# Attention of a batch in three visits of both head halves by a third of the tokens, in place of four of one half by one half; the last numerators left to the next tile

## Chip, cores, metric

One core of one Trainium2 chip. The metric is the device time of one execution in microseconds (us); lower is better.

## The reference

Attention over keys and values pooled in eights, followed by a gated feed-forward block over all tokens. Tokens 4608, model width 512, hidden width 2048.

```python
# shortened
k_p = k.reshape(8, 8, 72, 8, 64).mean(axis=3)       # batch, head, pooled row, 8, 64
v_p = v.reshape(8, 8, 72, 8, 64).mean(axis=3)
scores = scale * np.matmul(q, k_p.transpose(0, 1, 3, 2))   # 576 x 72 per head
attn = np.exp(scores - max)
attn = attn / (np.sum(attn, axis=-1, keepdims=True) + 1e-09)
x = (attn @ v_p) -> tokens x 512
h = x @ w_in;  g = h * sigmoid(h);  out = g @ w_out
```

## The kernel before

The tokens pass in nine tiles of 512. Each tile has a first half ("up": x @ w_in, SiLU) and a second half ("down": the product with w_out). From tile 1 on, both halves use a seven-product scheme in place of eight; that is where the sums on DVE come from. Attention of batch t+1 is put into the second half of tile t: a list of pieces, each with a position, and between large product number i-1 and i of that half the pieces with position up to i are emitted. Every engine works its own list in the order of emission.

A piece of attention is one of three groups of small matmuls. Four of them sit side by side in the array, as each uses 32 rows or 32 columns.

```python
def scores(b, g, f):            # g: half of the heads, f: half of the tokens
    sc = [ps_tile([128, 512], FP32, "at", "sc_ps")[:SP, :HS] for s in range(4)]
    for c in range(2):
        for s in range(4):
            rows = slice(32 * s, 32 * (s + 1))
            nc.tensor.matmul(sc[s], lhsT=kz[b % 2][rows, g, c, :],
                rhs=st["qT"][rows, g, f * QF : (f + 1) * QF, c, :], ...)
    es = mid.tile([SP, 4, HS], BF16, tag="es", bufs=4, name="es")
    for s in range(4):
        nc.scalar.activation(es[:, s, :], sc[s], func=AF.Exp, scale=score_scale)
# denominators(b, g, f): 4 matmuls of 288 columns with ones, then 1/x as exp(-ln x) on ACT
# numerators(b, g, f):   8 matmuls of 288 columns, then 2 multiplications by 1/x on DVE into xT
...
q_at = [15, 16, 17, 49] if t > 1 else [24, 25, 26, 49] if t else [82, 84, 86, 88]
# the first three q transposes stand in "up", the fourth (position 49) in "down"
f_down.append((10, lambda: pool_v(a)))                       # tiles 2 on: additions for v
...
for stage in range(2):
    f_down.append((100, lambda stage=stage: pool_k(a + 1, stage)))   # additions for k
f_up.append((0, lambda: load_q(a + 1)))
f_up.append((1, lambda: load_one(a + 1, "k")))     # first half of the rows, from SyncE
f_up.append((2, lambda: load_rest(a + 1, "k")))    # second half added by the DMA, from GpSimd
f_down.append((11, lambda: load_one(a + 1, "v")))
f_down.append((12, lambda: load_rest(a + 1, "v")))
...
visits = [(f, g) for f in range(2) for g in range(2)]
sc_at, den_at, nu_at = (1, 28, 56, 77), (28, 46, 69, 89), (46, 69, 89, 93)   # tiles 1 to 6
sc_at, den_at, nu_at = (1, 14, 22, 30), (14, 22, 30, 38), (42, 47, 52, 57)   # tile 0
```

k and v are summed in eights: the first half of the rows is loaded by SyncE's queue, the second is added to it by an accumulating DMA from GpSimd (which waits for the first), and three additions on DVE do the rest.

The softmax here doesn't subtract the row's maximum and nothing guards it: scores larger than these inputs give would overflow.

## Time and profile before

| | before |
|---|---|
| time, median | 290.5 us (290.41 to 291.13) |
| PE busy | 281.2 of 288.6 us |
| matmuls recorded | 2578 |
| DVE busy | 226.8 us |

How to read it: PE is the bound, so a change helps if it takes time from PE or fills a stop of PE. DVE, busy four fifths of the time, is the engine whose order can stop PE. The lines are in the prediction. A **visit** is one run of small matmuls between large ones. A **lap** is the time from the first large product of one tile's second half to that of the next tile's; laps leave out the start, whose length differs by about 1 us between runs of any kernel (see the last section).

### The profile page before, as it was taken

To read this page: it belongs to the slowest core of one execution; us is meant where nothing else is said; L and a number is where in the kernel's file an instruction comes from. 1 tells how busy PE (TensorE), PEld (TensorE's weight loads), DVE (VectorE), ACT (ScalarE), POOL (GpSimd) and SP (SyncE) were. 2 spreads that over 40 slices of the span, in tenths; PEclk is the share of its full clock that TensorE was granted. 3 is DMA by queue.
4 is the path that set the end of the run, shared out by engine and by line. 5 is a ranking of instruction groups with operands and counts; after the bars stand their busy time and mean duration, and the time that the engine had idled before them with its cause. 6 is when DMAs were issued, how large, how long until landed. Compare 5 with 4: busy or idle time off the path is not lost.

```text
span 288.6 us, 6600 instructions
## 1 busy us (share of the span) xinstructions
PE 281.2 (97%) x2578; PEld 189.9 (66%) x2597; DVE 226.8 (79%) x417; ACT 187.9 (65%) x401; POOL 52.2 (18%) x68
## 2 busy tenths in 40 slices
PE   7989999999999999999999999999999999999995
PEld 2448434465667676657788767676777667786684
DVE  4986844989789796979698879887988876746783
ACT  1768675568656877578767866786679657425700
POOL 8744316501020011101200106203000000000000
PEclk9999999999999999999999999999999999999999
DMA  7999999893758565875995495979830023005004
GB/s 214 276 278 215 232 301 151 221 206 55 145 82 187 127 91 76 133 179 123 137 182 166 61 138 81 164 156 163 149 82 2 2 65 83 1 2 140 6 2 145
DMA packets 35295, 37.67 MB, mean 131 GB/s; under 512 B 9952, under 2 KB 27616, under 8 KB 35264
## 3 DMA queue, kind: packets, MB, share of 16 engines
q0 software_dynamic: 21760, 20.86, 43.3%
q1 hardware_dynamic: 12928, 15.48, 22.0%
q10 hardware_dynamic: 576, 0.92, 0.9%
q8 instruction: 20, 0.33, 0.5%
q14 instruction: 11, 0.09, 0.1%
HBM read 36.70 MB, written 9.44 MB: 160 GB/s over the span
## 4 chain that ended last, share of the span: by engine, by line
PE 91%; DVE 2%; ACT 2%; DMA 2%; issue 1%; DVEq 0%
PE hp_ps L518 24%; PE o_psP L623 15%; PE o_psQ L623 15%; PE u_psQ L460 6%; PE u_psP L460 6%; PE o_psR L623 5%; PE o_ps L550 4%; PE sc_ps L330 4%; PE nu_ps L370 3%; PE den_ps L347 3%; PE u_psR L460 2%; DMA raw<-in_k_dram 2%; PE warm_ps L672 1%; ACT es L338 1%; PE kz_ps L295 1%
## 5 line engine op out<-in xcount | busy, mean ns | idle before, releaser
L518 PE MATMUL hp_ps<-xT,w_in_sb 128*128 128x512 bf16 (+3 forms) x398 | 80.5, 338 | 1.2 <-ACT h_T L524 0.4
L524 ACT ACTIVATE h_T<-hp_ps 128x512 bf16<-128x512 f32 (+2 forms) x95 | 51.4, 545 | 33.1 <-PE hp_ps L518 31.9
L623 PEld LDWEIGHTS <-h_sum 128*128 128x128 bf16 x640 | 60.4, 98 | 15.2 <-issue 6.1
L583 DVE TENSOR_TENSOR h_sum<-h_T 128x1024 bf16<-128x1024 bf16 (+1 forms) x72 | 50.9, 743 | 7.0 <-ACT h_T L524 7.0
L518 PEld LDWEIGHTS <-w_in_sb 128*128 128x128 bf16 x412 | 39.3, 98 | 24.9 <-issue 1.5
L338 ACT ACTIVATE es<-sc_ps 72x288 bf16<-72x288 f32 x128 | 41.4, 402 | 12.6 <-PE sc_ps L330 12.5
L378 DVE TENSOR_TENSOR xT<-nu_ps,rec 128x288 bf16<-128x288 f32 x64 | 25.8, 450 | 13.2 <-PE nu_ps L370 13.0
L460 PEld LDWEIGHTS <-w_sum 128*128 128x128 bf16 x300 | 29.3, 98 | 7.7
L623 PEld LDWEIGHTS <-h_T 128*128 128x128 bf16 x256 | 23.5, 98 | 6.7 <-issue 4.3
L468 ACT ACTIVATE h_T<-c_sb 128x512 bf16<-128x512 f32 x30 | 18.8, 628 | 10.8 <-DVE c_sb L492 10.8
L152 DVE STREAM_TRANSPOSE qT<-q_bf 128x576 bf16<-128x576 bf16 x32 | 22.9, 753 | 0.0
L181 POOL DMA_DIRECT2D raw<-in_k_dram x5 | 7.0, 1405 | 75.1 <-DVE h_sum L583 37.7
L356 ACT ACTIVATE lnd<-den_ps 128x288 f32<-128x288 f32 x30 | 12.3, 411 | 10.8 <-PE nu_ps L370 5.8
L273 DVE TENSOR_TENSOR raw<-raw 128x384 f32<-128x384 f32 (+3 forms) x20 | 12.4, 619 | 8.0 <-DMA raw<-in_v_dram 4.4
L623 PE MATMUL o_psP<-w_out_sb,h_sum 128*128 128x256 bf16 x128 | 17.6, 273 | 0.0
L623 PE MATMUL o_psQ<-w_out_sb,h_sum 128*128 128x256 bf16 x128 | 17.6, 273 | 0.0
L623 PE MATMUL o_psQ<-w_sum,h_T 128*128 128x256 bf16 x128 | 17.5, 274 | 0.0
L623 PE MATMUL o_psP<-w_sum,h_sum 128*128 128x256 bf16 x128 | 17.0, 273 | 0.0
L623 PE MATMUL o_psR<-w_sum,h_sum 128*128 128x256 bf16 x128 | 16.7, 273 | 0.0
L623 PE MATMUL o_psP<-w_sum,h_T 128*128 128x256 bf16 x128 | 16.7, 273 | 0.0
L530 POOL DMA_DIRECT2D out_dram<-o_sb x1 | 0.6, 628 | 82.3 <-issue 82.3
L623 PE MATMUL o_psQ<-w_sum,h_sum 128*128 128x256 bf16 x128 | 15.4, 273 | 0.0
(77 smaller groups left out, 426.8 us busy)
## 6 DMA issues: line engine op xcount, KB each, us to landing
out_dram<-o_sb SPq DMA_DIRECT2D x128, 64.0 KB, 2.5
q_bf<-in_q_dram POOLq DMA_DIRECT2D x6, 576.0 KB, 11.4
raw<-in_k_dram SPq DMA_DIRECT2D x6, 512.0 KB, 5.5
raw<-in_k_dram POOLq DMA_DIRECT2D x5, 576.0 KB, 8.8
raw<-in_v_dram POOLq DMA_DIRECT2D x5, 576.0 KB, 8.7
raw<-in_v_dram SPq DMA_DIRECT2D x5, 512.0 KB, 6.4
w_in_sb<-in_moe_w_in_dram POOLq DMA_DIRECT2D x8, 256.0 KB, 8.7
w_out_sb<-in_moe_w_out_dram POOLq DMA_DIRECT2D x4, 512.0 KB, 13.5
```

The costliest lines, as they stand in the source:

```text
L152: nc.vector.transpose(out=st["qT"][:, a, f * QF : (f + 1) * QF].rearrange("r i c p -> r (i c p)"), in_=st["q_bf"][:, a, f * n : (f + 1) * n],)
L273: nc.vector.tensor_add(out=raw[..., :w], in0=raw[..., :w], in1=raw[..., w : 2 * w])
L330: nc.tensor.matmul(sc[s], lhsT=kz[b % 2][rows, g, c, :], rhs=st["qT"][rows, g, f * QF : (f + 1) * QF, c, :], start=(c == 0), stop=(c == 1),)
L338: nc.scalar.activation(es[:, s, :], sc[s], func=AF.Exp, scale=score_scale)
L356: nc.scalar.activation(lnd, den_ps[:, :HS], func=AF.Ln)
L378: nc.vector.tensor_mul(out=xT[:, 2 * g + c, cols], in0=nu[c][:, :HS], in1=rec)
L460: nc.tensor.matmul(ps[bank][:, u, :], lhsT=w[:, kk, 128 * u : 128 * (u + 1)], rhs=x[:, kk, :], start=first and u == 0 and kk == 0, stop=kk ...
L468: nc.scalar.activation(h_T[:, g : g + 2, j * NQ : (j + 1) * NQ], src, func=AF.Silu)
L518: nc.tensor.matmul(hp_ps[:, r0:r1], lhsT=w_in_sb[:, kk, g * 128 : (g + 1) * 128], rhs=xT[:, kk, x0 : x0 + r1 - r0], start=(kk == 0), stop= ...
L524: nc.scalar.activation(h_T[:, g, n0 : n0 + n], hp_ps[:, :n], func=AF.Silu)
L583: nc.vector.tensor_tensor(out=h_sum[n][:, ks, :], in0=quarter(*a, ks), in1=quarter(*b, ks), op=op)
L623: nc.tensor.matmul(ps[b][:, c, :], lhsT=left(n, kt, c), rhs=W_OUT[n][:, kt, :], start=b not in begun, stop=kt == k1 - 1, skip_group_check= ...
```

## The change

Intent: each batch needs three scores, three denominators and three numerators in place of four of each. A visit handles both head halves of a third of the tokens: scores 16 matmuls of 192 columns, denominators 4 of 384, numerators 16 of 192. Where two groups meet at one position they share a visit, and the numerators of the last third are put behind the first numerators of the next tile. The middle third needs the last quarter of q, so that transpose moves up from 49 to 8.

```diff
+    QV = QI // 3
+    def third(n):
+        return tuple((g, n * QV, (n + 1) * QV) for g in range(2))
-    def scores(b, g, f):
+    def scores(b, segs):
...
-    visits = [(f, g) for f in range(2) for g in range(2)]
+    visits = [third(n) for n in range(3)]
...
-            q_at = [15, 16, 17, 49] if t > 1 else [24, 25, 26, 49] if t else [82, 84, 86, 88]
+            q_at = [15, 16, 17, 8] if t > 1 else [24, 25, 26, 8] if t else [82, 84, 86, 88]
...
-                f_to.append((q_at[n], lambda n=n: q_transpose(a, n // 2, n % 2)))
+                f_to.append((q_at[n], lambda n=n: q_transpose(a, n % 2, n // 2)))
...
-                sc_at, den_at, nu_at = (1, 28, 56, 77), (28, 46, 69, 89), (46, 69, 89, 93)
+                sc_at, den_at, nu_at = (1, 31, 75), (31, 56, 97), (56, 97, 101)
             else:
-                sc_at, den_at, nu_at = (1, 14, 22, 30), (14, 22, 30, 38), (42, 47, 52, 57)
+                sc_at, den_at, nu_at = (1, 16, 30), (16, 30, 44), (44, 55, 56)
...
-                if n < 3 or not 3 <= t < B - 2:
+                if n < 2 or not 0 < t < B - 2:
...
-                if n == 0 and 3 < t < B - 1:
-                    f_down.append((nu_at[n], lambda: numerators(a - 1, 1, 1)))
+                if n == 0 and 1 < t < B - 1:
+                    f_down.append((nu_at[n], lambda: numerators(a - 1, visits[2])))
```

More of the change, by code (lines that the diff above doesn't have):

```diff
@@ L69 @@
     DH = D // 2
+    VW = max(HS, 2 * S // 3)
     score_scale = float(1.0 / (D ** 0.5) / POOL)
@@ L320, in copy_v, with part, width, seg_cols @@
         copy(out=batches[b]["vp"][:, hs, :], in_=batches[b]["v_ps"][:SP, hs, :])
-    def scores(b, g, f):
-        st = batches[b]
-        sc = [ps_tile([128, 512], FP32, "at", "sc_ps")[:SP, :HS] for s in range(4)]
-        for c in range(2):
-            for s in range(4):
-                rows = slice(32 * s, 32 * (s + 1))
-                nc.tensor.matmul(
-                    sc[s],
-                    lhsT=kz[b % 2][rows, g, c, :],
-                    rhs=st["qT"][rows, g, f * QF : (f + 1) * QF, c, :],
-                    start=(c == 0), stop=(c == 1),
-                )
-        es = mid.tile([SP, 4, HS], BF16, tag="es", bufs=4, name="es")
+    def part(g, f):
+        return ((g, f * QF, (f + 1) * QF),)
+    QV = QI // 3
+    def third(n):
+        return tuple((g, n * QV, (n + 1) * QV) for g in range(2))
+    def width(segs):
+        return QP * sum(i1 - i0 for _, i0, i1 in segs)
+    def seg_cols(segs):
+        o = 0
+        for g, i0, i1 in segs:
+            n = QP * (i1 - i0)
+            yield g, i0, i1, slice(o, o + n)
+            o += n
+    def scores(b, segs):
+        st = batches[b]
+        w = width(segs)
+        sc = [ps_tile([128, 512], FP32, "at", "sc_ps")[:SP, :w] for s in range(4)]
+        for g, i0, i1, cs in seg_cols(segs):
+            for c in range(2):
+                for s in range(4):
+                    rows = slice(32 * s, 32 * (s + 1))
+                    nc.tensor.matmul(
+                        sc[s][:, cs],
+                        lhsT=kz[b % 2][rows, g, c, :],
+                        rhs=st["qT"][rows, g, i0:i1, c, :],
+                        start=(c == 0), stop=(c == 1),
+                    )
+        es = mid.tile([SP, 4, VW], BF16, tag="es", bufs=4, name="es")[:, :, :w]
         for s in range(4):
             nc.scalar.activation(es[:, s, :], sc[s], func=AF.Exp, scale=score_scale)
-        st[f"es{g}{f}"] = es
-    def denominators(b, g, f, on_dve=False):
+        st["es", segs] = es
+    def denominators(b, segs, on_dve=False):
         st = batches[b]
-        es = st[f"es{g}{f}"]
+        w = width(segs)
+        es = st["es", segs]
         den_ps = ps_tile([128, 512], FP32, "at", "den_ps")
@@ L347, in denominators, with numerators @@
             nc.tensor.matmul(
-                den_ps[32 * s : 32 * (s + 1), :HS],
+                den_ps[32 * s : 32 * (s + 1), :w],
                 lhsT=ones, rhs=es[:, s, :], start=True, stop=True,
             )
-        rec = mid.tile([128, HS], FP32, tag="rec", bufs=4, name="rec")
+        rec = mid.tile([128, VW], FP32, tag="rec", bufs=4, name="rec")[:, :w]
         if on_dve:
-            nc.vector.reciprocal(rec, den_ps[:, :HS])
+            nc.vector.reciprocal(rec, den_ps[:, :w])
         else:
-            lnd = mid.tile([128, HS], FP32, tag="lnd", name="lnd")
-            nc.scalar.activation(lnd, den_ps[:, :HS], func=AF.Ln)
+            lnd = mid.tile([128, VW], FP32, tag="lnd", name="lnd")[:, :w]
+            nc.scalar.activation(lnd, den_ps[:, :w], func=AF.Ln)
             nc.scalar.activation(rec, lnd, func=AF.Exp, scale=-1.0)
-        st[f"rec{g}{f}"] = rec
-    def numerators(b, g, f, tags=("at", "at")):
+        st["rec", segs] = rec
+    def numerators(b, segs, tags=("at", "at")):
         st = batches[b]
-        c0 = b * S % NX + f * HS
-        cols = slice(c0, c0 + HS)
-        es = st.pop(f"es{g}{f}")
-        rec = st.pop(f"rec{g}{f}")
+        w = width(segs)
+        g0, i0, i1 = segs[0]
+        c0 = b * S % NX + i0 * QP
+        cols = slice(c0, c0 + (i1 - i0) * QP)
+        es = st.pop(("es", segs))
+        rec = st.pop(("rec", segs))
         nu = []
@@ L368, in numerators @@
             nu_ps = ps_tile([128, 512], FP32, tags[c], "nu_ps")
-            for s in range(4):
-                nc.tensor.matmul(
-                    nu_ps[32 * s : 32 * (s + 1), :HS],
-                    lhsT=st["vp"][:, 4 * g + s, c::2],
-                    rhs=es[:, s, :],
-                    start=True, stop=True,
-                )
+            for g, _, _, cs in seg_cols(segs):
+                for s in range(4):
+                    nc.tensor.matmul(
+                        nu_ps[32 * s : 32 * (s + 1), cs],
+                        lhsT=st["vp"][:, 4 * g + s, c::2],
+                        rhs=es[:, s, cs],
+                        start=True, stop=True,
+                    )
             nu.append(nu_ps)
+        ng = len(segs)
         for c in range(2):
             nc.vector.tensor_mul(
-                out=xT[:, 2 * g + c, cols], in0=nu[c][:, :HS], in1=rec
+                out=xT[:, 2 * g0 + c : 2 * (g0 + ng - 1) + c + 1 : 2, cols],
+                in0=nu[c][:, :w].rearrange("r (g n) -> r g n", g=ng),
+                in1=rec.rearrange("r (g n) -> r g n", g=ng),
             )
@@ L712 @@
     q_transpose(0, 0, 0)
-    scores(0, 0, 0)
+    scores(0, part(0, 0))
     slot_sums("k", 1)
@@ L719 @@
     warm_up(2)
-    scores(0, 1, 0)
-    denominators(0, 0, 0)
+    scores(0, part(1, 0))
+    denominators(0, part(0, 0))
     slot_sums("v", 0)
@@ L725 @@
     copy_v(0, 0, act_copy)
-    denominators(0, 1, 0)
+    denominators(0, part(1, 0))
     q_transpose(0, 0, 1)
-    scores(0, 0, 1)
+    scores(0, part(0, 1))
     slot_sums("v", 1)
     warm_up(1)
-    numerators(0, 0, 0, ("mm", "at"))
+    numerators(0, part(0, 0), ("mm", "at"))
     warm_up(2)
@@ L736 @@
     warm_up(2)
-    numerators(0, 1, 0, ("mm", "at"))
-    scores(0, 1, 1)
+    numerators(0, part(1, 0), ("mm", "at"))
+    scores(0, part(1, 1))
     warm_up(2)
@@ L764 @@
             items += [(g, 0, NTT) for g in range(GA, KG)]
-            f_up += [(1, lambda: denominators(0, 0, 1, on_dve=True))]
-            f_up += [(5, lambda: denominators(0, 1, 1, on_dve=True))]
-            f_up += [(13, lambda: numerators(0, 0, 1))]
-            f_up += [(17, lambda: numerators(0, 1, 1))]
+            f_up += [(1, lambda: denominators(0, part(0, 1), on_dve=True))]
+            f_up += [(5, lambda: denominators(0, part(1, 1), on_dve=True))]
+            f_up += [(13, lambda: numerators(0, part(0, 1)))]
+            f_up += [(17, lambda: numerators(0, part(1, 1)))]
         else:
@@ L843 @@
             if t:
-                sc_at, den_at, nu_at = (1, 28, 56, 77), (28, 46, 69, 89), (46, 69, 89, 93)
+                sc_at, den_at, nu_at = (1, 31, 75), (31, 56, 97), (56, 97, 101)
             else:
-                sc_at, den_at, nu_at = (1, 14, 22, 30), (14, 22, 30, 38), (42, 47, 52, 57)
-            for n, (f, g) in enumerate(visits):
-                f_down.append((den_at[n], lambda f=f, g=g: denominators(a, g, f)))
-                f_down.append((sc_at[n], lambda f=f, g=g: scores(a, g, f)))
-            for n, (f, g) in enumerate(visits):
-                if n < 3 or not 3 <= t < B - 2:
-                    at = nu_at[n] + 2 * (t == 1 and n == 0)
-                    f_down.append((at, lambda f=f, g=g: numerators(a, g, f)))
-                if n == 0 and 3 < t < B - 1:
-                    f_down.append((nu_at[n], lambda: numerators(a - 1, 1, 1)))
+                sc_at, den_at, nu_at = (1, 16, 30), (16, 30, 44), (44, 55, 56)
+            for n, sg in enumerate(visits):
+                f_down.append((den_at[n], lambda sg=sg: denominators(a, sg)))
+                f_down.append((sc_at[n], lambda sg=sg: scores(a, sg)))
+            for n, sg in enumerate(visits):
+                if n < 2 or not 0 < t < B - 2:
+                    f_down.append((nu_at[n], lambda sg=sg: numerators(a, sg)))
+                if n == 0 and 1 < t < B - 1:
+                    f_down.append((nu_at[n], lambda: numerators(a - 1, visits[2])))
         moe_tables()
```

## The prediction

> **What bounds the kernel now.** I read the page first, then the busy time of each engine by stretch, then the order of instructions in time for one tile, then who waited for whom.
>
> ```profile
> PE 281.2 (97%) x2578; PEld 189.9 (66%) x2597; DVE 226.8 (79%) x417; ACT 187.9 (65%) x401; POOL 52.2 (18%) x68
> PE 91%; DVE 2%; ACT 2%; DMA 2%; issue 1%; DVEq 0%
> ...
> 188.20:204.60 16.40, 16.38 (x192) 12.01 (x192) 13.45 (x22) 12.78 (x30) 2.82 (x2) 1.00 0.80 145
> 247.60:260.00 12.40, 12.40 (x113) 10.84 (x113) 7.00 (x11) 3.23 (x5) 0.00 (x0) 1.00 0.03 6
> ```
>
> PE is busy 97%, and the chain that ended last is 91% PE: outside the start, PE is never idle for long. The two stretches are the second half ("down") of a tile with attention in it (16.40 us) and of one without (12.40 us). Attention of one batch costs PE about 4 us, seven times. So only PE's own time and waits that stop PE count; fewer ACT or DVE instructions are worth nothing in themselves.
>
> The order in time says what those 4 us are. Large products (L623) follow each other every 0.109 us (eight from 189.38 to 190.25).
>
> ```profile
> 188.02 0.38 PE L623 MATMUL o_psP<-w_out_sb,h_sum 128*128 128x256 bf16 x2
> 188.34 0.44 PE L330 MATMUL sc_ps<-qT,kz 32*72 32x288 bf16 x8
> 188.71 0.83 PE L623 MATMUL o_psP<-w_out_sb,h_sum 128*128 128x256 bf16 x6
> 189.38 1.04 PE L623 MATMUL o_psQ<-w_out_sb,h_sum 128*128 128x256 bf16 x8
> ...
> 191.76 0.31 PE L347 MATMUL den_ps<-es,ones 72*32 72x288 bf16 x4
> 192.00 0.44 PE L330 MATMUL sc_ps<-qT,kz 32*72 32x288 bf16 x8
> ...
> 194.44 0.31 PE L347 MATMUL den_ps<-es,ones 72*32 72x288 bf16 x4
> 194.57 0.66 PE L370 MATMUL nu_ps<-es,vp 72*32 72x288 bf16 x16
> 195.17 0.28 PE L623 MATMUL o_psR<-w_sum,h_sum 128*128 128x256 bf16 x1
> ```
>
> Four small matmuls run at once: 16 numerators (four groups of 4) take 195.17 - 194.57 = 0.60 us, and eight of them elsewhere 198.74 - 198.39 = 0.35, so a group of 288 columns takes 0.122 us and leaving costs 0.1. The scores put in at 188.24 (188.02 plus two products) end at 188.71: 0.47 us, of which two groups are 0.245. The other **0.225 us is the price of going from large products to small ones and back**. Denominators followed by scores cost about 0.11 more (194.57 - 194.44 = 0.13 from denominators to numerators, but 0.24 to scores). The seven insertions of this tile cost 0.47, 0.70, 0.82, 0.47, 0.58, 0.48 and 0.59 = 4.11 us, of which the streams are 2.45.
>
> **What the Trainium skill says.** "TensorEngine Tiling (Array Packing)", Tiling Modes, states that changing the tiling mode drains TensorE: the trace agrees, 0.225 us per visit. "TensorE: Matmul & The Clock Gate", Part 3, says that tiles of different row groups run at once; the trace agrees (0.44 us in all for eight scores). The same page, Part 2, Back-to-back issue gap, gives N / 2.4 + 2.5 ns for one warm matmul: 122.5 ns at 288 columns, as the groups here show; for 192 and 384 columns I use it as an estimate, 82.5 and 162.5 ns. "PSUM — Partial Sum Buffer", Engine vs sequencer instructions, states that the VectorE queue is strictly first in, first out. The DVE rows below agree: each group begins where the one before it ends, so a transpose queued behind other work waits for it.
>
> **The change part by part.** The streamed columns stay. Per batch: scores 8 groups of 288 become 12 of 192, numerators the same, denominators 4 of 288 become 3 of 384. Streams before 20 x 0.1225 = 2.45 us, after 24 x 0.0825 + 3 x 0.1625 = 2.47: 0.02 x 7 = +0.14 us in all.
>
> Insertions fall. The built order has, for tiles 0 to 6, 9, 9, 8, 7, 7, 7, 8 runs of small matmuls in "down" before and 6, 5, 5, 5, 5, 5, 6 after: 18 fewer, 18 x 0.225 = -4.05. One passage from denominators to scores also goes: -0.11. **PE's own work: -4.0 us.** ACT and DVE have fewer, longer instructions (exp 402 ns for 288 columns); off the path, nothing.
>
> Three waits take some of it back.
>
> *Tile 1, the moved q transpose.* The middle third needs the last quarter of q, so its transpose moves from position 49 to 8, and scores of that third stand at 31. In tile 1 it is queued behind the four additions for v (L273, L277), themselves behind a backlog:
>
> ```profile
> 69.52 2.49 DVE L583 TENSOR_TENSOR h_sum<-h_T 128x1024 bf16<-128x1024 bf16 x4
> 71.93 0.55 DVE L273 TENSOR_TENSOR raw<-raw 128x384 f32<-128x384 f32 x1
> 72.52 0.36 DVE L277 TENSOR_TENSOR v<-raw 128x192 bf16<-128x192 f32 x1
> 72.80 0.42 DVE L273 TENSOR_TENSOR raw<-raw 128x256 f32<-128x256 f32 x1
> 73.25 0.29 DVE L277 TENSOR_TENSOR v<-raw 128x128 bf16<-128x128 f32 x1
> 73.46 0.68 DVE L638 TENSOR_TENSOR rr_sb<-o_psQ,r_sb 128x512 f32<-128x512 f32 x1
> ```
>
> The transpose would begin at 73.46 and be done 0.77 later, 74.2 with its signal 74.3. The second scores stand at 72.03 before; three products later (0.33), with a longer stream before them (0.13), their second half is wanted at 72.03 + 0.46 + 0.2 = 72.7. PE stands still for **1.6 us**. In tiles 2 to 6 the additions for v come after it: in the tile at 188.02 it would end at 191.41 + 0.77 = 192.18 and be wanted at 192.6. No wait, with 0.3 us to spare.
>
> *Tile 0.* From 48.6 on DVE is full to the end (a copy 0.6, eight weight sums of 0.335, the last multiplications 0.37 apart). After, the eight sums stand ahead of all four last multiplications (384 columns: 0.465 apart, an estimate, 0.1 more for 96 columns), and their last ends near 53.8, where before it ended at 54.2. PE would arrive 0.7 earlier, at 52.8, and needs them for its first products: it waits about 0.75 and the tile's saving is gone: **+0.75**.
>
> *Tiles 2 to 6, first half.* In tiles 2 and 3 a chain already stops PE near 94.7 and 124.8: multiplications late in "down", k sums, x sums, rr_sb, t_sb, three transposes, c_sb, ACT's copy, rr_sb.
>
> ```profile
> 90.53 2.09 DVE L152 STREAM_TRANSPOSE qT<-q_bf 128x576 bf16<-128x576 bf16 x3
> 92.54 0.65 DVE L492 TENSOR_TENSOR c_sb<-u_psP,t_sb 128x512 f32<-128x512 f32 x1
> 93.12 0.67 DVE L496 TENSOR_TENSOR c_sb<-u_psQ,t_sb 128x512 f32<-128x512 f32 x1
> 94.36 0.69 DVE L480 TENSOR_TENSOR rr_sb<-u_psQ,r_sb 128x512 f32<-128x512 f32 x1 [0.57 <-ACT r_sb L477]
> ```
>
> There the k sums start 0.57 us before the end of "down" (84.94 against 85.52); in later tiles 1.16 before (203.47 against 204.63), with no stop. After the change the last multiplications stand at position 97 in every tile, 14 products (1.53 us) plus some 0.7 from the end. They begin 1.5 before it, take 0.93, and the k sums start about 0.56 before it, as in tiles 2 and 3. So tiles 4, 5 and 6 get the stop of 0.3 too: **+0.9**.
>
> Sum: -4.0 + 1.6 + 0.75 + 0.9 = **-0.75 us; 290.5 becomes 289.8.**
>
> **The rivals.**
> 1. *PE's work alone*: no new waits, 290.5 - 4.0 = 286.5. For it: PE is the bound and has few waits now. Against: the DVE rows above, saturated where the changed order leans on it. A part is likely, if the backlog in tile 1 is shorter than before.
> 2. *Narrow groups cost as much as wide ones* (the weight load or the issue of 8 instructions as the bound): 24 x 0.04 x 7 = +6.7 us, so about 296.5. Against: the 12 small v matmuls of 64 columns at 73.72 take 0.6 us with loads of their own, and eight scores issue within 0.15 us.
> 3. *The transposes are late in every tile*, not in tile 1 alone: each 0.1 us beyond the margin of 0.3 costs 0.5 us in five tiles; a further 0.5 us late would give 292.
> 4. *ACT's longer exps delay denominators*: 4 x 0.08 = 0.3 us against three products' delay of 0.33: tight in tiles 2 to 6, perhaps 0.5 us in all.
>
> **Range and chances.** Two per cent is 5.8 us, more than the whole PE saving, so faster needs a mechanism that I don't see; slower by as much needs rival 2 in full. Between, the three waits are worth 3.25 us and each may be off by half: 288.2 to 291.4 should hold it 8 times in 10. Faster 0.02, same 0.96, slower 0.02.
>
> **What would show it.** PE's matmuls rise by 196. Groups of 192 columns 0.08 us apart, and some 3.7 us of insertions in a late "down" where 4.1 stood, show the PE side right. A gap before scores in tile 1, ended by the DVE transpose, of 1.6 us; hp_ps at the start of tile 1 waiting for xT; u_psQ waiting for rr_sb in tiles 2 to 6. Groups at 0.12 us would prove the prediction wrong upwards; no transpose wait, downwards.

## The result and the profile after

Changed 291.21 us median (290.33 to 292.44, six runs), before 291.04 us on the same chip (290.41 to 291.45, six runs): ratio 1.0004, 95% interval 0.9984 to 1.0025, **the same time**. A ratio is the mean of one kernel's fast runs over the mean of the other's of the same rounds, so it isn't quite the ratio of the medians.

The page of the changed kernel, busy time and the chain that ended last:

```profile
PE 280.9 (97%) x2793; PEld 195.9 (68%) x2793; DVE 225.6 (78%) x403; ACT 183.4 (63%) x359; POOL 52.3 (18%) x68
...
PE 87%; DVE 7%; ACT 3%; issue 1%; DMA 1%; SPq 0%; DVEq 0%
```

The chain has moved: PE 87% where it was 91%, DVE 7% where it was 2%. PE's work shrank, and waits for DVE came in. The laps show where (us; "again" is a second profile of the same changed kernel, the last column the repaired version at the end of the experiments):

| lap | before | changed | again | four repairs |
|---|---|---|---|---|
| 0 (second half of tile 0, first half of tile 1) | 33.71 | 33.64 | 33.64 | 33.09 |
| 1 | 31.15 | 31.51 | 31.51 | 30.13 |
| 2 | 30.10 | 29.36 | 29.36 | 29.10 |
| 3 | 29.38 | 29.40 | 29.40 | 29.18 |
| 4 | 29.54 | 29.37 | 29.38 | 29.10 |
| 5 (second half of tile 5, first half of tile 6) | 29.54 | 30.47 | 30.09 | 29.10 |
| 6 | 29.88 | 29.51 | 29.52 | 29.52 |
| sum | 213.30 | 213.26 | 212.90 | 209.22 |

The work did fall: weight loads, one to each matmul (some records of matmuls are missing), went from 2597 to 2793, the 196 that the prediction gives, while PE's busy time fell. The changed kernel's second half of tile 5, PE in order of time (start, duration, count):

```profile
188.32 0.38 PE L651 MATMUL o_psP<-w_out_sb,h_sum 128*128 128x256 bf16 x2
188.63 0.53 PE L351 MATMUL sc_ps<-qT,kz 32*72 32x192 bf16 x16
189.09 0.83 PE L651 MATMUL o_psP<-w_out_sb,h_sum 128*128 128x256 bf16 x6
...
194.96 1.15 PE L651 MATMUL o_psP<-w_sum,h_T 128*128 128x256 bf16 x9
196.03 0.35 PE L369 MATMUL den_ps<-es,ones 72*32 72x384 bf16 x4
196.21 0.83 PE L395 MATMUL nu_ps<-es,vp 72*32 72x192 bf16 x32
196.97 0.94 PE L651 MATMUL o_psP<-w_sum,h_T 128*128 128x256 bf16 x7
```

The scores cost 189.09 - 188.32 - 2 x 0.109 = 0.55 us, as 0.225 + 4 x 0.0825 says. The visit at 196.03, with two batches' numerators in it, costs 196.97 - 194.96 - 9 x 0.109 = 1.03. The five visits take 0.55 + 0.825 + 1.03 + 0.55 + 0.70 = 3.66 us where seven took 4.11.

What took it back are stops of PE. **Tile 1**, changed kernel, PE and DVE:

```profile
73.22 0.36 PE L351 MATMUL sc_ps<-qT,kz 32*72 32x192 bf16 x8
...
74.07 0.29 DVE L278 TENSOR_TENSOR v<-raw 128x128 bf16<-128x128 f32 x1
74.28 0.77 DVE L153 STREAM_TRANSPOSE qT<-q_bf 128x576 bf16<-128x576 bf16 x1
...
75.11 0.36 PE L351 MATMUL sc_ps<-qT,kz 32*72 32x192 bf16 x8 [1.52 <-DVE qT L153]
```

Half of the scores run, the other half waits for the transpose that stands behind the additions for v. By start times of the matmuls the stop is 1.68 us.

**Tile 0**, second half, first the kernel before, then the changed one:

```profile
47.56 1.25 PE L550 MATMUL o_ps<-w_out_sb,h_T 128*128 128x512 bf16 x5
48.74 0.43 PE L370 MATMUL nu_ps<-es,vp 72*32 72x288 bf16 x8
49.10 1.25 PE L550 MATMUL o_ps<-w_out_sb,h_T 128*128 128x512 bf16 x5
```

```profile
48.34 0.82 PE L578 MATMUL o_ps<-w_out_sb,h_T 128*128 128x512 bf16 x3
49.78 1.89 PE L578 MATMUL o_ps<-w_out_sb,h_T 128*128 128x512 bf16 x8 [0.62 <-ACT o_sb L586]
```

Before, numerators stood between the first three quarters of the output and the last one, and covered ACT's copy that frees a PSUM bank. Now PE waits for that copy: 0.78 us by start times. At the start of tile 1, where the prediction put this stop, PE waits 0.04 us.

**First halves of tiles 2 to 6**: 0.22 to 0.29 us between the products into u_psP and u_psQ, as in tiles 2 and 3 before; the second group would follow the first by 0.44 us without a stop:

```profile
95.54 0.69 DVE L508 TENSOR_TENSOR rr_sb<-u_psQ,r_sb 128x512 f32<-128x512 f32 x1 [0.57 <-ACT r_sb L505]
95.58 0.60 PE L488 MATMUL u_psP<-x_sum,w_in_sb 128*128 128x256 bf16 x4
...
96.29 0.60 PE L488 MATMUL u_psQ<-x_sum,w_in_sb 128*128 128x256 bf16 x4
```

**Tile 6, not foreseen.** Before, then changed; DVE's first addition for k, and the products into u_psR that need what DVE does next:

```profile
203.47 1.21 DVE L187 TENSOR_TENSOR raw<-raw 72x1024 f32<-72x1024 f32 x1
...
207.01 0.60 PE L460 MATMUL u_psR<-x_sum,w_sum 128*128 128x256 bf16 x4
```

```profile
204.72 1.22 DVE L188 TENSOR_TENSOR raw<-raw 72x1024 f32<-72x1024 f32 x1 [1.01 <-DMA raw<-in_k_dram]
...
207.72 0.61 PE L488 MATMUL u_psR<-x_sum,w_sum 128*128 128x256 bf16 x4 [0.69 <-DVE x_sum L455]
```

k's addition waits 1.01 us for a load that was in time before. By start times PE stops 0.86 us. All listed stops of the changed kernel sum to 0.78 + 1.68 + (0.27 + 0.27 + 0.22 + 0.27 + 0.29) + 0.86 = 4.64 us, against 2 x 0.29 = 0.58 before: 4.06 us given back. The laps changed by -0.04, so PE's own work fell by 4.1 us, worked out as this difference.

### The profile page after: what moved, and what is told of

It reads as the page before. It is cut to its first block, busy times and chain, and to the rows that moved or that the text cites. A ratio compares the mean times of both kernels' runs of the same rounds, so it can differ in the third digit from the quotient of the medians.

```text
span 289.5 us, 6939 instructions
## 1 busy us (share of the span) xinstructions
PE 280.9 (97%) x2793; PEld 195.9 (68%) x2793; DVE 225.6 (78%) x403; ACT 183.4 (63%) x359; POOL 52.3 (18%) x68
## 4 chain that ended last, share of the span: by engine, by line
PE 87%; DVE 7%; ACT 3%; issue 1%; DMA 1%; SPq 0%; DVEq 0%
PE hp_ps L546 21%; PE o_psP L651 14%; PE o_psQ L651 14%; PE u_psQ L488 6%; PE u_psP L488 5%; PE o_psR L651 5%; PE o_ps L578 5%; PE warm_ps L700 4%; PE sc_ps L351 4%; PE nu_ps L395 3%; PE u_psR L488 2%; PE den_ps L369 2%; DVE h_sum L611 1%; DVE w_sum L629 1%; DVE qT L153 1%; DVE rr_sb L508 1%
## 5 line engine op out<-in xcount | busy, mean ns | idle before, releaser
L546 PE MATMUL hp_ps<-xT,w_in_sb 128*128 128x512 bf16 (+3 forms) x412 | 82.6, 340 | 0.4 <-ACT h_T L552 0.4
L546 PEld LDWEIGHTS <-w_in_sb 128*128 128x128 bf16 x412 | 39.3, 98 | 24.9 <-issue 1.5
L359 ACT ACTIVATE es<-sc_ps 72x384 bf16<-72x384 f32 (+1 forms) x100 | 39.1, 470 | 11.0 <-PE sc_ps L351 10.9
L404 DVE TENSOR_TENSOR xT<-nu_ps,rec 128x384 bf16<-128x384 f32 (+1 forms) x50 | 24.0, 533 | 2.1 <-PE nu_ps L395 1.9
L378 ACT ACTIVATE lnd<-den_ps 128x384 f32<-128x384 f32 (+1 forms) x23 | 11.1, 484 | 21.2 <-PE den_ps L369 21.2
L651 PE MATMUL o_psQ<-w_sum,h_sum 128*128 128x256 bf16 x128 | 16.7, 273 | 0.0
L651 PE MATMUL o_psQ<-w_out_sb,h_sum 128*128 128x256 bf16 x128 | 16.6, 273 | 0.0
L651 PE MATMUL o_psP<-w_sum,h_T 128*128 128x256 bf16 x128 | 16.5, 273 | 0.0
L651 PE MATMUL o_psQ<-w_sum,h_T 128*128 128x256 bf16 x128 | 16.5, 273 | 0.0
L578 PE MATMUL o_ps<-w_out_sb,h_T 128*128 128x512 bf16 x64 | 15.5, 380 | 0.6 <-ACT o_sb L586 0.6
L651 PE MATMUL o_psR<-w_sum,h_sum 128*128 128x256 bf16 x128 | 15.7, 273 | 0.0
L488 PEld LDWEIGHTS <-w_in_sb 128*128 128x128 bf16 x120 | 11.7, 97 | 5.7 <-issue 1.7
## 6 DMA issues: line engine op xcount, KB each, us to landing
w_out_sb<-in_moe_w_out_dram POOLq DMA_DIRECT2D x4, 512.0 KB, 13.7
```

The lines of the kernel that those rows point to most:

```text
L404: nc.vector.tensor_mul(out=xT[:, 2 * g0 + c : 2 * (g0 + ng - 1) + c + 1 : 2, cols], in0=nu[c][:, :w].rearrange("r (g n) -> r g n", g=ng), ...
L488: nc.tensor.matmul(ps[bank][:, u, :], lhsT=w[:, kk, 128 * u : 128 * (u + 1)], rhs=x[:, kk, :], start=first and u == 0 and kk == 0, stop=kk ...
L546: nc.tensor.matmul(hp_ps[:, r0:r1], lhsT=w_in_sb[:, kk, g * 128 : (g + 1) * 128], rhs=xT[:, kk, x0 : x0 + r1 - r0], start=(kk == 0), stop= ...
L578: nc.tensor.matmul(ps, lhsT=h_T[:, g, m * 128 : (m + 1) * 128], rhs=w_out_sb[:, g, :], start=(g == 0), stop=(g == KG - 1),)
L651: nc.tensor.matmul(ps[b][:, c, :], lhsT=left(n, kt, c), rhs=W_OUT[n][:, kt, :], start=b not in begun, stop=kt == k1 - 1, skip_group_check= ...
```

## The experiments

The question is where 4.1 us went and whether the stops are the change's own. My theory: the four stops, each repairable by itself. Rivals: the k stop is luck of one profile; repairs only move the waits. Times such as +6.0 us below count from the start of the second half of the tile named.

### Again, unchanged

> The changed kernel once more, unchanged. My theory of the result: PE's own work did fall (by about 2 us over tiles 1 to 6, plus the first-half gaps it already fills), and four stops of PE took it back: 1.7 us in tile 1 ahead of the middle scores (DVE transpose behind the additions for v), 0.6 in tile 0 (a PSUM bank freed by ACT's copy), four times 0.27 in the first halves of tiles 2 to 5, and 1.1 in tile 6, where the k additions waited for the last accumulate load of k. If all four belong to the change, this profile shows the first large product of tile 6's first half to its second half at 14.4 to 14.6 us again, with a DVE k addition waiting on the load of k for about 1 us, and the ratio to the kernel before is 1.000 within 0.003. Rival: the tile 6 stop is the luck of one profile (a late DMA); then that half takes 13.4 us here and no k addition waits.

291.25 us, ratio 1.0003 (0.9977 to 1.0028). Lap 5 is 30.09, and a k addition waited for its load again, 0.63 us (PE 0.48). The stop is not luck, though its size varies. Over the five fast profiles with this order of loads in tile 5 it was 1.01, 0.63, 1.01, 1.13 and 0.17 us of DVE.

### Tile 1: the transpose first

```diff
-            q_at = [15, 16, 17, 8] if t > 1 else [24, 25, 26, 8] if t else ...
+            q_at = [15, 16, 17, 8] if t > 1 else [24, 25, 26, 7] if t else ...
-            f_down.append((33, lambda: hidden_sum(7, 0, 8)))
+            f_down.append((33 if t > 1 else 49, lambda: hidden_sum(7, 0, 8)))
# tile 1 also: select_v 40 -> 46, copy_v 41 -> 47, middle scores and first denominators 31 -> 33
```

> The changed kernel with tile 1 alone reordered: the last q transpose ahead of the additions for v instead of behind them (the selections of v, the hidden sum 7 and the middle scores a little later to make room). Theory: the 1.7 us stop ahead of the middle scores of tile 1 goes, and the second half of tile 1 falls from 18.08 to 16.4 us; 1.6 us faster than the changed kernel (ratio 0.9945 to it and to the kernel before). Rival, another wait takes its place (the v additions are now later and the selections of v or the numerators wait): under 0.5 us.

289.48 us, ratio 0.9944 (0.9926 to 0.9962); lap 1 went from 31.51 to 30.13. The timeline of this version:

```profile
71.92 0.77 DVE L153 STREAM_TRANSPOSE qT<-q_bf 128x576 bf16<-128x576 bf16 x1
...
72.66 0.53 PE L351 MATMUL sc_ps<-qT,kz 32*72 32x192 bf16 x16
```

The transpose ends in time, the 16 scores run in one piece. This stop was worth 1.4 us by laps and 1.7 by time. In the profile a k addition also waited 0.35 us in tile 4 (lap 4 took 29.82 where 29.37 stood): the rival, a new wait, came true in part, though not in the place expected.

### The last batch's k loads ahead of its q loads

```diff
-                f_up.append((0, lambda: load_q(a + 1)))
+                f_up.append((0 if a + 1 < B - 1 else 3, lambda: load_q(a + 1)))
```

> The changed kernel with one DMA order changed: for the last batch the eight loads of q are issued after the loads of k instead of ahead of them. Theory: k's accumulate load lands before the k additions of tile 6 are reached, so no k addition waits and the first half of tile 6 takes 13.3 to 13.5 us instead of 14.53; 1.1 us faster than the changed kernel, ratio 0.996. Rival one, luck of one profile: no difference in the time. Rival two, the loads are held by the stores ahead of them whatever their order: half 14.5 again.

290.07 us, ratio 0.9969 (0.9944 to 0.9994). Lap 5 is 29.36: the stop is gone. But in the profiled run (292.0 us) a k addition of another tile waited 2.35 us, for a load that this edit doesn't touch:

```profile
146.62 1.22 DVE L188 TENSOR_TENSOR raw<-raw 72x1024 f32<-72x1024 f32 x1 [2.35 <-DMA raw<-in_k_dram]
```

So k's loads are near the edge in several tiles, and a late one can cost a run 2 us or more (lap 3 took 31.84 us here, where 29.40 stood).

### Tile 0: numerators back at 44, 47, 52

```diff
-                sc_at, den_at, nu_at = (1, 16, 30), (16, 30, 44), (44, 55, 56)
+                sc_at, den_at, nu_at = (1, 16, 30), (16, 30, 44), (44, 47, 52)
```

> The changed kernel with tile 0 alone reordered: the last two numerators at positions 47 and 52 of the second half, as in the kernel before, instead of 55 and 56. My prediction's reading: PE stops at the start of tile 1 because the last multiplications stand behind the weight sums on DVE. The trace's reading: PE stops 0.62 us before the last eight large products of tile 0, for a PSUM bank that ACT's copy frees, since no small products stand there any more. In both, this order gives back 0.6 to 0.7 us (ratio 0.998); they are told apart by where the stop was: with the trace's reading the stop before the last eight products is under 0.1 here and the first product of tile 1 waits under 0.1 as well in both kernels. Rival: the stop only moves (the numerators wait for their denominators at 47): no gain.

The time says nothing: 292.27 us, ratio 1.0023 (0.9994 to 1.0052), but three of its six runs, the profiled one too, had a granted clock of 0.992 to 0.994 (in the trace, a dip to half the clock at 75.4 to 78.9 us). The other three took 290.48, 290.5 and 291.87. The stage isn't touched by the dip: lap 0 went from 33.64 to 33.09.

```profile
49.29 0.51 PE L395 MATMUL nu_ps<-es,vp 72*32 72x192 bf16 x16
49.98 1.24 PE L578 MATMUL o_ps<-w_out_sb,h_T 128*128 128x512 bf16 x4 [0.17 <-ACT o_sb L586]
```

The numerators stand in the gap again, and 0.17 us of the wait for ACT's copy is left. The trace's reading holds, and my prediction's (xT late because DVE is full) does not: in the changed kernel PE waits 0.04 us for the multiplications at most.

### One more visit per tile

```diff
-                    f_down.append((nu_at[n], lambda: numerators(a - 1, visits[2])))
+                    f_down.append((nu_at[n] + 3, lambda: numerators(a - 1, visits[2])))
```

> The changed kernel with the numerators that were left to the next tile put in by themselves three products later, instead of right behind that tile's first numerators: one more visit of PE to small matmuls in each of the tiles 2 to 6, nothing else. Theory of the prediction: each visit costs 0.225 us, so the second halves of tiles 2 to 5 grow from 15.94 to 16.17 us (16.2 with DVE on its heels), +1.1 us in all, ratio to the changed kernel 1.004. Rival: the price is in the streams and not in the visits; then under 0.3 us in all.

291.64 us, ratio 1.0025 (0.9994 to 1.0055). Laps 2, 3 and 6 grew by 0.23, 0.22 and 0.22 us, each with one visit more and nothing else. In laps 4 and 5 the k loads blur it, as longer tiles give them more time in lap 5. The price of a visit, 0.22 us, is confirmed by itself, in the laps; the timed runs are too noisy to resolve 1 us.

### The kernel before with only the transpose moved

```diff
-            q_at = [15, 16, 17, 49] if t > 1 else [24, 25, 26, 49] if t else ...
+            q_at = [15, 16, 17, 8] if t > 1 else [24, 25, 26, 8] if t else ...
```

> The kernel before with one part of the change alone: the last q transpose of tiles 1 to 6 at position 8 of the second half instead of 49. The scores that need it still stand at 77, so no stop in tile 1. Theory for the stop in tile 6: the transpose now runs ahead of the additions for v on DVE, so v's buffer comes free 0.66 us later, the load of v is issued at +6.0 us of tile 5's second half instead of +5.35, and the accumulate load of k, whose bytes move behind v's, lands at +15.5 to +16.5 instead of +14.5; the k addition then waits for it and tile 6's first half grows from 13.2 us by 0.3 to 1.0. Time against the kernel before: +0.1% to +0.3%. Rival: the late landing comes from the stores that the changed kernel issues 1.1 us earlier at the end of tile 5; then k lands at +14.5 to +15.2 here and no k addition waits.

293.46 us, ratio 1.0082 (1.0057 to 1.0108): slower by more than I expected, and PE lost it elsewhere. Laps 1, 4, 5 and 6 grew by 0.66, 0.47, 0.49 and 0.48: in tile 1 numerators wait for v, and in the later tiles the third scores take 0.93 us where 0.44 stood. No k addition waited. But the loads did what the theory said. The views of DMA issues, 20 us around the second half of tile 5, first the kernel before, then this one (the last number is the time from issue to landing):

```profile
raw<-in_k_dram POOLq DMA_DIRECT2D x1, 576.0 KB, 7.6
```

```profile
raw<-in_k_dram POOLq DMA_DIRECT2D x1, 576.0 KB, 9.1
```

v was issued at +6.0 us in place of +5.35, and k landed at +15.6 in place of +14.5. The rival was that the late landing comes from the output stores, which the changed kernel issues 1.1 us earlier, from +14.46 on. Here the first store went out at +16.0, after k had landed, so the stores are not needed for this much of the delay. k was in time only because the tile had become longer and DVE came to k at +15.9, not +15.45.

### Three repairs together

> The changed kernel with the three repairs together: tile 1's transpose ahead of the additions for v, the last batch's k loads ahead of its q loads, tile 0's numerators at 44, 47 and 52. Theory: the stops are independent, since each ends before the next tile begins, so they add: -1.7 -1.0 -0.55 = -3.2 us, ratio 0.989 to the kernel before (287.9 us). Rival: the saving is taken up by a further wait behind each, at most the -1.7 of tile 1's repair alone is seen (ratio 0.994).

288.76 us, ratio 0.9932 (0.9905 to 0.9958): 2.0 us better than the kernel before, not 3.2. Laps 0, 1 and 5 gained what each repair alone gave. Lap 2 was 0.92 longer, as k's addition waited 0.82 us for its load in tile 2. A new wait had taken the place of an old one. That it came because tiles 0 and 1 had become shorter is not shown: with tile 1's repair alone the same load landed at +13.1, in time, and here at +16.2, in one profile each.

### Three repairs, and the additions for k earlier

```diff
-                    f_down.append((100, lambda stage=stage: pool_k(a + 1, stage)))
+                    f_down.append(((72, 84)[stage] if t > 1 else 100, lambda ...))
```

> The three repairs and the k additions of tiles 2 to 5 moved from position 100 to 72 and 84 of the second half, ahead of the last multiplications on DVE. Theory: the stop of 0.27 us between the first two products of the unit in the first halves of tiles 3 to 6 goes: -1.1 us more than the three repairs alone, ratio 0.985 (286.8 us). Rival: the k load has not landed by position 72 in some tiles, DVE waits for it and holds up the multiplications behind it: the same as the three repairs or up to 1 us worse.

297.95 us over all six runs, three of them in the slow state at a clock of 0.977 to 0.988. The ratio of the fast ones is 1.0141 (1.0093 to 1.019), but these (293.32, 295.34 and 297.08 us) had a clock of 0.986 to 0.994 as well, so its size is not to be read as the price of the waits; the trace is. The rival was right: asked for earlier, k isn't there.

```profile
143.31 1.22 DVE L188 TENSOR_TENSOR raw<-raw 72x1024 f32<-72x1024 f32 x1 [4.65 <-DMA raw<-in_k_dram]
```

DVE works in order, so the copy of a PSUM bank behind it waits as well, and PE stops 3.9 us. In laps 4 and 5, where k was there or late by 0.76 us of DVE's time alone, the stop of 0.27 us in the first half was gone: 29.10 and 29.15.

### v's loads 34 products later

> The changed kernel with the loads of v issued 34 products later (position 45 and 46 of the second half instead of 11 and 12), so after the start of k's accumulate load in every tile. The run before this one (the kernel before with the transpose moved) showed v's issue going from +5.35 to +6.0 us and k's last landing in tile 5 from +14.5 to +15.6. If k's bytes do queue behind v's, k lands at +12.5 or earlier in tile 5 here, no k addition of tiles 2 to 6 waits for a load, and tile 6's first half is 13.2 to 13.5 us instead of 13.9 to 14.5: 0.7 to 1.1 us faster than the changed kernel, ratio to the kernel before 0.997. Rival: k's landing is set by its own issue and by q's loads of the last batch; then it lands at +15 to +16.4 again.

A failed experiment: 291.86 us, ratio of the five fast runs 1.0014 (0.9973 to 1.0055); the sixth, the profiled one, was slow (321.68 us, clock 0.851). The two kernels proved to be the same program on every engine. SyncE has no large products in its list, so a later position among them changes nothing: v's load goes out when its buffer is free. It counts as one more timing of the changed kernel.

### k's first loads from GpSimd

```diff
-        load_rows(nc.sync, raw, source(b, name)[:, :, :PH])
+        load_rows(nc.gpsimd if name == "k" else nc.sync, raw, source(b, name)[:, :, :PH])
-                f_up.append((0, lambda: load_q(a + 1)))
+                f_up.append((3, lambda: load_q(a + 1)))
```

> The changed kernel with k's plain loads issued from GpSimd instead of from the queue of SyncE, where they stand behind 16 stores for some 14 us; q's loads after k's. k's accumulate load should then be issued some 5 to 8 us earlier in every tile and land before +8 us of the second half: no k addition waits, tile 6's first half 13.2 to 13.5 us, ratio 0.997. Rival: GpSimd's own queue makes q late, and the q transposes at the start of tiles 3 to 6 hold up the first half by more than that.

290.32 us, ratio 0.9970 (0.9948 to 0.9993), and all six runs within 290.08 to 290.64. No k addition waits; lap 5 is 29.37. In SyncE's queue 16 stores stand ahead of k's first load and take about 14 us to go out (173.41 to 187.34 in the changed kernel). Out of it, and ahead of q's loads, k's accumulating load of tile 5 is issued at -3.7 us where it was +7.2, and lands at +6.3. The edit moves both at once, so it does not say what each is worth.

### Three repairs with the early k, and four

> The earlier k loads together with the repairs of tiles 0 and 1. The former set of three repairs was 2.0 us faster than the changed kernel and not 3.2, as its k load was late in tile 2 (0.8 us). With k early in every tile: -1.7 -0.55 -0.9 = -3.1 us to the changed kernel, ratio 0.9895 to the kernel before (288.0 us).

288.10 us (five runs), ratio 0.9894 (0.9870 to 0.9917), as expected.

> The same with the k additions of tiles 2 to 5 at positions 72 and 84, where they failed before for want of the loaded k (a stop of 3.9 us in tile 3). With k early they don't wait; the stop of 0.27 us in the first halves of tiles 3 to 6 goes, -1.1 us more: ratio 0.9857 (286.9 us). If DVE's own work is the reason for those stops and not k's place in it, no gain beyond the three.

286.98 us (286.60 to 287.06, four runs), **ratio 0.9852** (0.9827 to 0.9877): the version that beats both. In it k's addition stands ahead of the last multiplications without a wait, and u_psQ follows u_psP at once:

```profile
122.52 0.60 PE L488 MATMUL u_psP<-x_sum,w_in_sb 128*128 128x256 bf16 x4
...
122.95 0.60 PE L488 MATMUL u_psQ<-x_sum,w_in_sb 128*128 128x256 bf16 x4
```

### v behind k in one queue

```diff
-        load_rows(nc.sync, raw, source(b, name)[:, :, :PH])
+        load_rows(nc.gpsimd if name == "v" else nc.sync, raw, source(b, name)[:, :, :PH])
```

> The changed kernel with v's plain loads issued from GpSimd, behind k's accumulate load in that queue, instead of from SyncE's queue, where they go out at +6.0 us of the second half. k's plain loads stay where they were. If v's bytes ahead of k's on the DMA engines are what makes k late, k's accumulate load, issued at +6 to +7 us in tile 5, lands before +14 us, no k addition waits, and tile 6's first half is 13.2 to 13.5 us: 0.7 to 1.1 us faster than the changed kernel, ratio to the kernel before 0.997. Rival: what comes ahead is q of the last batch or the stores; then k lands at +15 to +16.4 us again and tile 6's first half takes 13.9 us or more.

290.29 us, ratio 0.9982 (0.9959 to 1.0006). The wait stayed (1.04 us, lap 5 at 30.50): k landed at +16.4. It didn't test what it should. The trace has the bytes of that queue at 132 to 194 KB per us from +11 to +16, some 770 KB, where k's load has 576: v's bytes moved alongside k's, not behind them.

### Control: the kernel before with early k

> The kernel before with the two repairs that concern k (plain loads from GpSimd, additions at 72 and 84 for tiles 2 to 5), as a control. It has no wait for a k load and stops of 0.29 us in tiles 2 and 3 only, of which the one in tile 3 can go: ratio 0.999 (290.8 us), between 0.997 and 1.001. Then nearly all of the 4.3 us between the version with four repairs and the kernel before belongs to the change. Rival: the earlier additions serve the kernel before as well, by 1 us or more (ratio 0.996 or less), and the change is worth that much less.

290.93 us, ratio 0.9994 (0.9972 to 1.0016; one run of the kernel before, of 566 us, is left out). Its lap 2 fell from 30.10 to 29.76 and the others stood. The early loads and additions are worth nothing to the kernel before that the timed runs resolve, so nearly all of the gain of the four repairs belongs to the change.

### The additions for v first, in tile 5 alone

```diff
-                f_down.append((10, lambda: pool_v(a)))
+                f_down.append((10 if t != 5 else 7, lambda: pool_v(a)))
```

> The changed kernel with the additions for v ahead of the last q transpose, in tile 5 alone. Two numbers. First, PE: the transpose now ends 1.9 us later, 1.6 us beyond its margin of 0.3, so the second half of tile 5 takes 17.5 us instead of 15.94, with the stop ahead of the second scores. Second, the loads: v goes out at +5.35 us and not +6.0; if that is what makes k late, k's last landing is at +14.5 to +15.0 us (plus up to 0.9 if an instruction fetch falls into it) instead of +16.0 to +16.5, and no k addition waits in tile 6. Rival: v's issue is not the cause; k lands at +15.8 us or later again.

One look, 291.88 us, of unknown state. What it undoes, first the kernel before, then the changed one, in the second half of tile 5:

```profile
191.41 1.21 DVE L187 TENSOR_TENSOR raw<-raw 72x1024 f32<-72x1024 f32 x1
...
193.37 1.17 SPq L172 DMA_DIRECT2D raw<-in_v_dram  x2
```

```profile
191.71 0.77 DVE L153 STREAM_TRANSPOSE qT<-q_bf 128x576 bf16<-128x576 bf16 x1
...
192.40 1.18 DVE L188 TENSOR_TENSOR raw<-raw 72x1024 f32<-72x1024 f32 x1
...
194.33 1.17 SPq L173 DMA_DIRECT2D raw<-in_v_dram  x2
```

Timeline of this version's tile 5, then the DMA views, first the changed kernel's, then this one's:

```profile
192.89 0.36 PE L351 MATMUL sc_ps<-qT,kz 32*72 32x192 bf16 x8
...
193.82 1.46 SPq L173 DMA_DIRECT2D raw<-in_v_dram  x2
...
194.53 0.36 PE L351 MATMUL sc_ps<-qT,kz 32*72 32x192 bf16 x8 [1.28 <-DVE qT L153]
```

```profile
raw<-in_k_dram POOLq DMA_DIRECT2D x1, 576.0 KB, 9.2
```

```profile
raw<-in_k_dram POOLq DMA_DIRECT2D x1, 576.0 KB, 7.8
```

v went out at 193.82, +5.35 us after the second half's start at 188.47. k's landing fell from 9.2 us after its issue in the changed kernel to 7.8 and came at +14.7 where it had been at +15.8 to +16.5. No k addition waited in tile 6; the longer tile would have excused a later landing (DVE came to k at +16.8), but +14.7 is ahead of the +15.4 at which DVE was ready for it in the changed kernel too. Both numbers came out as expected: PE's stop ahead of the scores is 1.44 us (expected 1.6).

One profile is little, but the others agree. Where k's accumulating load was issued at +5.5 to +7.3 us, it landed at +14.5 to +14.8 in the three cases with v at +5.35 (tiles 3 and 5 before, tile 5 here) and at +15.2 to +16.5 in the ten with v at +6.0, over all traces but that of v behind k, where v goes another way. **So this much is shown: the moved transpose pushes the additions for v back by 0.66 us, v's buffer comes free later, v's load moves into the way of k's, and k's margin (+14.5 against +15.4, 0.9 us before) is all but gone or gone.** The Trainium skill, "DMA: Bandwidth & Descriptors", Issuing engines are not separate DMA queues, says that DMAs from ScalarE, SyncE and GpSimd run on the same 16 DMA engines and interleave. These traces agree as far as they go: in tile 5 of the kernel before, v's bytes (issued by SyncE) fall from 225 KB in the us at +8 to 92 at +9 and none at +10, while k's (issued by GpSimd) rise from 47 at +9 to 110 and 140.

What stays open is the last part of the lateness. A load gives 16 landing signals. In the changed kernel 15 of them had come at +15.2 us, just ahead of DVE at +15.4, and the last at +16.4, so in that profile the whole wait hangs on the last one. Two rivals were not tested. The first output stores go out at +14.46 there, before k has landed; in the kernel before, in the version with only the transpose moved and in this one they go out at +15.6 to +16.0, after it, and the last signal comes within 0.2 us of the one before. And a 16 KB instruction fetch of 0.89 us began at +14.3 and may have held that one engine; against it, a fetch of 1.04 us fell in the same place here (+13.7) without a late last signal.

## Why the prediction was right and wrong

It forecast -0.75 us with a range that holds the result; the measured change is +0.04% (within the noise). The direction was not borne out, and one wait was missing from the sum.

- **PE's own work, -4.0**: right, -4.1 by laps and stops; and the group of 192 columns (0.0825), the visit's price (0.225, measured alone as 0.22) and the 3.7 us of insertions were each right.
- **Tile 1, +1.6**: right, 1.68, and taking it away gave 1.4 to 1.7 back.
- **Tile 0, +0.75**: the size was right (0.78) by luck, the mechanism wrong. I had DVE's last multiplications stop the first products of tile 1. What stopped was the bank that ACT frees, four products earlier, as the moved numerators no longer covered its copy.
- **Tiles 4 to 6, first halves, +0.9**: right, 0.22 + 0.27 + 0.29 = 0.78, and gone when the k additions move ahead of the multiplications.
- **The failing step: "In tiles 2 to 6 the additions for v come after it [...] No wait, with 0.3 us to spare."** It asked only whether the transpose is in time for PE. It did not ask what the additions it pushes back set free: v's buffer, v's load, and through the shared DMA engines k's load. That term was missing, and k's wait measured 0.86 us of PE (0.48 in the second profile). With 0.86 the sum is +0.1. That v's later load takes k's margin is shown; why the last landing signal comes later still is open.
- Rivals: 1 (PE alone, 286.5) failed for the changed kernel as built, but 286.98 is what it takes once its stops are repaired. 2 (narrow groups as dear as wide ones) is refuted by 0.0825. 3 (the transpose late everywhere) did not occur; it takes the additions for v ahead of it to make 1.44 us. 4 (ACT's longer exps) did not show.

## What to carry to other kernels

When an instruction moves up in an engine's order, ask what those it passes were about to set free, not only whether its own reader is served: a buffer freed 0.66 us later delayed a load, and that load another one. When the bound engine loses work in several places, list what the removed instructions were covering (here a copy that frees a bank), and expect the gain only after each covered wait has its new cover. And when a repair makes a stage shorter, look again at the loads with a deadline in the next.

## What the Trainium skill lacked or had wrong

- "TensorEngine Tiling (Array Packing)", Tiling Modes: it says that a change of mode drains TensorE and gives no price. Here a visit to 32-wide tiles and back cost 0.22 us, alone, in three laps, and denominators followed by scores 0.1 more.
- "TensorE: Matmul & The Clock Gate", Part 2, Back-to-back issue gap: it puts streams of weight load and matmul at about 131 ns per matmul at N = 512 and says that the formula N / 2.4 + 2.5 over-counts there. Here 512-column products with a weight load each follow at 216 ns and 256-column ones at 109 ns, the formula's 215.8 and 109.2.
- The same page, Part 1: it gives about 3.4 us to a warm clock with a transition point that varies by 0.5, and in another sentence 6 to 14 cold matmuls for one kernel. The runs fit the second and not the first: the first products of 512 columns followed each other at 427 ns for about 2.9 us (7 products) in two profiles (the kernel before, the changed one again) and for 5.5 to 6 us (13 and 14) in two others (the changed kernel, the tile 0 repair), and at 216 ns from then on, with the same start-up code. The first large product of tile 0 came at 17.05 and 17.09 against 17.95 and 18.14 us: about 1 us of difference between runs that no part of the change makes.
- "DMA: Bandwidth & Descriptors", Anatomy of one DMA: its fit, 2.0 us + bytes / 436 KB per us, would be 3.4 us for 576 KB. No page gives a figure for accumulating loads: here the five of k in the kernel before took 7.6 to 10.1 us from issue to landing, beside other traffic, and moved 131 to 143 KB per us while no other queue moved data (+11 to +14 us of tile 5).
